# Turning a weight matrix by DMA instead of on TensorE, and what has to move for it: a gated MLP with a complex recurrence on one core

## The chip, the core and the metric

One core of one Trainium2 chip. The metric is the device time of one execution in microseconds (us). A kernel's time is the median of several executions. Engines: PE is TensorE, DVE is VectorE, ACT is ScalarE, POOL is GpSimd, SP is SyncE, which here only issues DMAs.

## The reference, cut to what matters

```python
def reference(x, Lambda_re, Lambda_im, B_re, B_im, C_re, C_im, log_dt, Dskip, w_gate, w_up, w_down):
    xn  = layernorm(x)                                   # x: 1 x 2048 x 448
    dt  = exp(log_dt);  Lam = Lambda_re + 1j*Lambda_im;  Lam_bar = exp(dt * Lam)
    Bu  = xn @ (((Lam_bar - 1) / Lam)[:, None] * (B_re + 1j*B_im)).T
    h_t = Lam_bar * h_(t-1) + Bu_t                       # over all 2048 tokens
    s   = 2 * real(h @ (C_re + 1j*C_im).T) + xn * Dskip
    g   = silu((silu(xn @ w_gate) * (xn @ w_up)) @ w_down)   # w_gate, w_up: 448 x 1792
    return x + s * g
```

## The kernel before

The tokens go in four quarters of 512 columns. Per quarter there are 14 blocks of 128 columns of `w_gate` and `w_up`, taken two at a time (a "pair": PSUM banks gp, up, gp, up). ACT empties them into `gs` and `us`, and DVE multiplies these into `Vt`. Then comes the projection Bu (banks pb and pk), the recurrence as a scan on DVE, `w_down` (bank hd) and the output sum (bank y). The recurrence is rotated by sine and cosine tables: DVE makes their phases (`table_phase`), ACT their values (`table_sin`).

In these traces an instruction that waits holds back those behind it on its engine (before the change ACT idles 1.84 us, until 23.47 us, for one of them with filled banks behind it), so the order of calls below *is* the schedule. The numbered lists are hooks: what is put into the queues behind the evictions of that pair.

```python
    for n in range(2):                      # two token tiles first
        ln_stats(n); ln_sqrt(n, n + 1); run_power()          # root: GpSimd power, then a reciprocal
    ...
    gu_matmuls(0, 0, begun, 0, W // 2, told=run_power)       # left token half of pair 0
    ...
    for d in range(0, KT, 2):
        b_transpose(0, d, nc.scalar)        # B_re: 16 PE transposes, copied out by ACT
    gu_matmuls(0, 0, begun, W // 2, W)      # right token half of pair 0
    ...
    gu(0, bg, 2.0, {
        0: [*stats(4, 5, 6, 7), *sqrt(1), on(params_in), on(table_phase, 0)],
        1: [*bs(1), on(b_clear), *rstd_of(1), *norms(4, 5, 6, 7), on(table_sin, 0)],   # bs: B_im
        2: [*transposes(4, 5, 6, 7), on(load_c), on(table_phase, 1), on(table_sin, 1),
            on(bu, 0, (0, 1)), on(table_phase, 2), on(table_sin, 2)],
        3: [on(bu, 0, (2,), "between"), on(table_phase, 3), on(table_sin, 3), on(params_fold)],
        4: [on(params_trig), on(ssm_steps, bg, 0)],
        5: [on(params_out)],
    }, begun)
```

Of the kernel before, what the change touches and what calls it, by code (L numbers as in the profile page):

```python
# [44 lines left out]
def kernel(  # L45
# [89 lines left out]


# [6 lines left out]
    def load_w(eng, eng2, dst, src, c0, c1):  # L143
        eng.dma_start(
            out=dst[:, 0:KF, c0:c1],
            in_=src[0 : KF * P, c0:c1].rearrange("(k p) f -> p k f", p=P),
        )
        eng2.dma_start(out=dst[:, KF, c0:c1], in_=src[blk(KF), c0:c1])

    def load_gu(c0, c1):  # L150
        load_w(nc.sync, nc.sync, Wg, B_w_gate, c0, c1)
        load_w(nc.sync, nc.sync, Wu, B_w_up, c0, c1)

    def load_nat(i, src):
        nc.sync.dma_start(
            out=nat[:, i, 0:KF, :], in_=src[0 : KF * P, :].rearrange("(k p) f -> p k f", p=P)
        )
        nc.sync.dma_start(out=nat[:, i, KF, :], in_=src[blk(KF), :])

    def load_turned(dst, src):  # L160

        for k, cols in ((slice(0, KF), slice(0, KF * P)), (slice(KF, KT), blk(KF))):
            nc.sync.dma_start(out=dst[:, k, :], in_=src[:, cols], transpose=True)

    nat = big.tile([P, 2, KT, D], BF16, name="nat", tag="vt")
# [19 lines left out]
    load_w(nc.sync, nc.sync, Wg, B_w_gate, 0, C0)  # L185
    load_w(nc.scalar, nc.scalar, Wu, B_w_up, 0, C0)
    load_nat(0, A_B_re)
    load_x(TQ, 2 * TQ)
    load_gu(C0, 768)
    load_nat(1, A_B_im)  # L190
    load_gu(768, F)

    nc.gpsimd.affine_select(
# [3 lines left out]
    halves = ctile([P, TQ], BF16, "halves")  # L197
    nc.gpsimd.memset(halves[:], 0.5)
    euler = ctile([P, KT], F32, "euler")
    nc.gpsimd.memset(euler[:], math.e)  # L200
    for r, v in enumerate((A_log_dt, A_Lambda_re, A_Lambda_im, A_Dskip)):
        nc.gpsimd.dma_start(out=vrow[r : r + 1, :], in_=v.unsqueeze(0))
# [21 lines left out]
    vep = ctile([P, NT], BF16, "vep")  # L224
    sd = ctile([P, NT], BF16, "sd")
# [10 lines left out]
    def ln_sqrt(n0, n1):  # L236
        power(sd[:, n0:n1], vep[:, n0:n1], halves[:, 0 : n1 - n0])

    def ln_rstd(n0, n1):
        nc.vector.reciprocal(out=rstd[:, n0:n1], in_=sd[:, n0:n1])  # L240
# [124 lines left out]
    def b_transpose(c, d, eng):  # L365

        tp = bank("tpb", BF16).rearrange("p (i w) -> p i w", i=2)
        for i in range(2):
            for k in (KF, *range(KF)):
                c0 = blk(k).start if c == 0 else (k + 1) % KT * P  # L370
                nc.tensor.transpose(  # L371
                    tp[:, i, c0 : c0 + P], nat[:, c, k, blk(d + i)], Id[:]
                )
        tp = tp[:, :, c * R : c * R + D]
        dst = BT[:, d : d + 2, c * D : (c + 1) * D]
        if eng is nc.scalar:
            nc.scalar.activation(dst, tp, ACT.Copy)
        else:
            nc.vector.tensor_copy(out=dst, in_=tp)

# [25 lines left out]
    SYNC = mybir.DependencyInfo(mybir.DependencyClass.Sync, mybir.DependencyReason.DATA)  # L406

# [9 lines left out]
    def sums(banks, weights, q, c0, c1, between=None, told=None):  # L417
# [3 lines left out]
        left = []  # L421
        for share, first in ((0, True), (1, False)):
            for n in range(len(banks)):
# [11 lines left out]
                if first:  # L435
                    left.append(tell(mm))
                    if told:
                        told()
                        told = None
# [5 lines left out]
    def bu(q, ns, packed=None):  # L445
# [15 lines left out]
        sums(pb, pairs, q, 0, W, between=whole if packed == "between" else None)  # L461
# [69 lines left out]
    def gu_banks():  # L531
        return [[bank("gp"), bank("up")] for _ in range(2)]

    def gu_matmuls(q, f0, banks, c0, c1, **kw):
        pairs = [[w[:, :, block(f)] for w in (Wg, Wu)] for f in (f0, f0 + 1)]
        sums(banks, pairs, q, c0, c1, **kw)

    def gu(q, bg, budget, hooks={}, begun=None):
# [3 lines left out]
        for f0 in range(0, NF, GRP):  # L542
# [3 lines left out]
            for i in range(0, n, 2):  # L546
                fi = f0 + i
                if begun and fi == 0:
                    banks = begun
                else:  # L550
                    banks = gu_banks()
                    gu_matmuls(q, fi, banks, 0, W)
                for j, (gp_, up_) in enumerate(banks):
                    nc.scalar.activation(gs[:, i + j, :], gp_[:], ACT.Silu)  # L554
                    nc.scalar.activation(us[:, i + j, :], up_[:], ACT.Copy)  # L555
# [54 lines left out]
    for n in range(2):  # L610
        ln_stats(n)
        ln_sqrt(n, n + 1)
        run_power()
    count_tokens()
    for n in range(2):
        ln_rstd(n, n + 1)
# [4 lines left out]
    warm(3)  # L621
    for n in range(2, TQ):
        ln_stats(n)
        ln_sqrt(n, n + 1)
    run_power()
    begun = gu_banks()
    gu_matmuls(0, 0, begun, 0, W // 2, told=run_power)
    for n in range(2, TQ):
        ln_rstd(n, n + 1)
        ln_norm(n)  # L630
    nc.scalar.activation(pcol[:], params_row(), ACT.Copy)
    ln_transpose(2, nc.vector)
    ln_transpose(3, nc.vector)
    power(dtv[:], euler[:], pcol[:, 0:KT, 0])
    for d in range(0, KT, 2):
        b_transpose(0, d, nc.scalar)
    gu_matmuls(0, 0, begun, W // 2, W)
    nc.sync.dma_start(out=Wd[:], in_=B_w_down.rearrange("(ft p) d -> p ft d", p=P))
    load_x(2 * TQ, NT)
# [11 lines left out]
    def sqrt(q):  # L651
        return [on(ln_sqrt, q * TQ, (q + 1) * TQ)]

    def rstd_of(q):
        return [on(ln_rstd, q * TQ, (q + 1) * TQ)]

    def bs(c):
# [85 lines left out]
```

## Time and profile before

| | before |
|---|---|
| median of 3 executions | 190.18 us (190.11 to 190.31) |
| span in the profile | 188.9 us (that execution took 190.72) |
| PE busy | 182.9 us, 97% |
| first gate/up matmul / end of pair 6 of quarter 0 | 7.85 us / 37.9 us |
| granted clock of PE | 1.00 |

From the page of the kernel before, the busy digits of three engines and the granted clock: the span in 40 slices of 4.7 us, tenths busy (9 is 90% or more); the first slice stands directly behind the name.

```profile
PE   7799999999999999999999999999999999999992
...
DVE  3889996799999999989999899789449999889253
ACT  3278599948999771107988632105996652302100
...
PEclk9999999999999999999999999999999999999999
```

PE's row has no hole after its second digit, so PE is the bound. DVE is nearly as full in the first half: a row of DVE put later there stays later. This row of the timeline (start us, us, engine, line, operation, tiles, idle before and what ended it) is the first step of the recurrence on DVE.

```profile
52.00 1.40 POOL L215 TENSOR_TENSOR sd<-vep,halves 128x4 bf16<-128x4 bf16 x1 [31.94 <-DVE vep L232]
```

```profile
34.00 1.23 DVE L498 TENSOR_TENSOR ere<-bu_re,CT 128x2048 bf16<-128x2048 bf16 x1 [2.33 <-ACT CT L306]
```

### The profile page before, as it was taken

The page shows a single profiled execution, that of the slowest core. Times are in us where ns is not written, and L with a number is a line of the kernel's source. Part 1 is how long each engine was busy: PE and PEld are TensorE (multiplying, and loading weights), DVE is VectorE, ACT ScalarE, POOL GpSimd, SP SyncE. Part 2 cuts the span into 40 slices and gives each one's busy share as a digit, 9 for nine tenths or more (in the row PEclk, how much of TensorE's full clock was granted, in tenths as well). Part 3 has the DMA queues.
Part 4 walks back from the last instruction along what each step waited for, and adds up shares of the span by engine and source line. Part 5 has one row for each costly group of instructions (what it writes and reads, how often), then busy time and mean ns, then how long its engine had stood idle before and what let it go on. Part 6 is the DMA issues. An engine that isn't in the chain of part 4 may idle for free.

```text
span 188.9 us, 3703 instructions
## 1 busy us (share of the span) xinstructions
PE 182.9 (97%) x1472; PEld 93.0 (49%) x1472; DVE 160.3 (85%) x267; ACT 104.0 (55%) x197; POOL 10.9 (6%) x21
## 2 busy tenths in 40 slices
PE   7799999999999999999999999999999999999992
PEld 3475434555555455544444455544444445555551
DVE  3889996799999999989999899789449999889253
ACT  3278599948999771107988632105996652302100
POOL 6422200000020000000020000000000000000000
PEclk9999999999999999999999999999999999999999
DMA  6999999100013100011005100020000000020020
GB/s 172 345 379 383 377 120 213 26 3 2 0 23 64 31 0 0 0 49 56 0 0 87 28 0 3 0 75 22 3 2 0 3 0 0 0 76 24 0 75 24
DMA packets 21121, 12.59 MB, mean 67 GB/s; under 512 B 11120, under 2 KB 20080, under 8 KB 21104
## 3 DMA queue, kind: packets, MB, share of 16 engines
q1 hardware_dynamic: 20288, 12.05, 24.3%
q10 hardware_dynamic: 688, 0.31, 0.6%
q8 instruction: 11, 0.18, 0.5%
q14 instruction: 6, 0.05, 0.1%
q0 software_dynamic: 128, 0.00, 0.0%
HBM read 8.03 MB, written 1.84 MB: 52 GB/s over the span
## 4 chain that ended last, share of the span: by engine, by line
PE 94%; DMA 2%; DVE 2%; ACT 0%; POOL 0%; issue 0%; SPq 0%; DVEq 0%
PE gp L428 24%; PE hd L567 23%; PE up L428 21%; PE y L582 11%; PE pb L428 10%; PE pk L453 2%; DMA x_all<-in_A_x_dram 2%; PE y L588 2%; PE tpb L371 1%; PE tp L259 1%; DVE ob L601 0%; DVE t L598 0%; DVE st L230 0%; ACT xT L261 0%; POOL sd L215 0%
## 5 line engine op out<-in xcount | busy, mean ns | idle before, releaser
L428 PE MATMUL gp<-xT,Wg 64*128 64x512 bf16 (+1 forms) x406 | 86.2, 369 | 0.1
L428 PE MATMUL up<-xT,Wu 64*128 64x512 bf16 (+1 forms) x406 | 85.9, 369 | 0.0
L428 PEld LDWEIGHTS <-Wg 64*128 64x128 bf16 x406 | 37.2, 94 | 23.8 <-issue 1.6
L428 PEld LDWEIGHTS <-Wu 64*128 64x128 bf16 x406 | 37.3, 94 | 19.5 <-POOLq L410 0.3
L567 PE MATMUL hd<-Wd,Vt 128*128 128x448 bf16 x224 | 43.2, 353 | 0.0
L554 ACT ACTIVATE gs<-gp 128x512 bf16<-128x512 f32 x56 | 35.1, 626 | 10.9 <-PE gp L428 7.5
L555 ACT ACTIVATE us<-up 128x512 bf16<-128x512 f32 x56 | 35.4, 633 | 0.0
L567 PEld LDWEIGHTS <-Vt 128*128 128x128 bf16 x224 | 21.8, 98 | 21.0 <-issue 0.8
L572 ACT ACTIVATE sg<-hd 128x448 bf16<-128x448 f32 x16 | 8.7, 543 | 38.3 <-PE hd L567 38.2
L559 DVE TENSOR_TENSOR Vt<-gs,us 128x2048 bf16<-128x2048 bf16 (+1 forms) x16 | 17.3, 1079 | 6.3 <-ACT us L555 6.3
L428 PE MATMUL pb<-xT,BT 64*128 64x512 bf16 x168 | 19.2, 376 | 0.0
L466 ACT ACTIVATE bu_re<-pb 128x512 bf16<-128x512 f32 x12 | 7.3, 611 | 20.9 <-PE pb L428 20.9
L598 DVE TENSOR_TENSOR t<-y,sg 128x448 f32<-128x448 f32 (+2 forms) x17 | 10.1, 595 | 10.0 <-PE y L582 9.6
L582 PE MATMUL y<-C,H_re 128*128 128x448 bf16 (+2 forms) x68 | 17.6, 342 | 0.0
L504 DVE TENSOR_TENSOR_SCAN bu_re<-rcol,H_re,ere 128x512 bf16<-128x512 f32 x12 | 15.1, 1268 | 0.0
L588 PE MATMUL y<-Dd,xT 128*128 128x128 bf16 x64 | 13.5, 212 | 0.0
L428 PEld LDWEIGHTS <-BT 64*128 64x128 bf16 x168 | 8.4, 94 | 10.1 <-issue 1.3
L582 PE MATMUL y<-C,H_im 128*128 128x448 bf16 (+2 forms) x51 | 11.9, 342 | 0.0
L230 DVE BATCH_NORM_STATS2 st<-x_all 128x6 f32<-128x448 bf16 x16 | 9.8, 616 | 2.0 <-DMA x_all<-in_A_x_dram 2.0
L504 DVE TENSOR_TENSOR_SCAN bu_im<-rcol,H_im,eim 128x512 bf16<-128x512 f32 x9 | 11.3, 1259 | 0.0
L601 DVE TENSOR_TENSOR ob<-t,x_all 128x448 bf16<-128x448 f32 (+2 forms) x17 | 10.2, 597 | 0.6
L215 POOL TENSOR_TENSOR sd<-vep,halves 128x1 bf16<-128x1 bf16 (+1 forms) x7 | 5.7, 813 | 77.8 <-PE up L428 41.8
(95 smaller groups left out, 174.9 us busy)
## 6 DMA issues: line engine op xcount, KB each, us to landing
out_dram<-ob SPq DMA_DIRECT2D x15, 112.0 KB, 1.7
Wd<-in_B_w_down_dram SPq DMA_DIRECT2D x1, 1568.0 KB, 12.0
x_all<-in_A_x_dram SPq DMA_DIRECT2D x1, 896.0 KB, 13.9
Wg<-in_B_w_gate_dram SPq DMA_DIRECT2D x1, 768.0 KB, 6.9
Wu<-in_B_w_up_dram SPq DMA_DIRECT2D x1, 768.0 KB, 8.2
x_all<-in_A_x_dram SPq DMA_DIRECT2D x1, 448.0 KB, 4.8
Wg<-in_B_w_gate_dram SPq DMA_DIRECT2D x1, 384.0 KB, 4.9
Wu<-in_B_w_up_dram SPq DMA_DIRECT2D x1, 384.0 KB, 5.3
```

Source lines behind the costliest of these rows:

```text
L230: nc.vector.bn_stats(out=st[:], in_=x_all[:, n, :])
L428: mm = nc.tensor.matmul(banks[n][i][:, c0:c1], lhsT=weights[n][i][h, d, :], rhs=xT[h, d, q * W + c0 : q * W + c1], start=(first and m == 0 ...
L504: nc.vector.tensor_tensor_scan(out=T["b"][c][:, k, :], data0=rcol[:, k : k + 1].to_broadcast([P, W]), data1=T["e"][c][:, k, :], initial=in ...
L554: nc.scalar.activation(gs[:, i + j, :], gp_[:], ACT.Silu)
L555: nc.scalar.activation(us[:, i + j, :], up_[:], ACT.Copy)
L559: nc.vector.tensor_tensor(out=Vt[:, f0 : f0 + n, :], in0=gs[:, 0:n, :], in1=us[:, 0:n, :], op=ALU.mult)
L567: nc.tensor.matmul(hd, lhsT=Vt_of[q][:, fi, j * P : (j + 1) * P], rhs=Wd[:, fi, :], start=(fi == 0), stop=(fi == NF - 1),)
L572: nc.scalar.activation(sg[:], hd, ACT.Silu)
L582: nc.tensor.matmul(y[:, c0:c1], lhsT=h, rhs=C2[:, n, c0:c1], start=(n == 0), stop=(n == NS - 1))
L588: nc.tensor.matmul(y[:, s + skip : s + P], lhsT=xT[:, n, m * P : (m + 1) * P], rhs=Dd[:, n, skip:P], start=False, stop=False,)
L598: nc.vector.tensor_tensor(out=t[:], in0=y, in1=sg[:, c0:c1], op=ALU.mult)
L601: nc.vector.tensor_tensor(out=ob[:], in0=t[:], in1=x_all[:, m, c0:c1], op=ALU.add)
```

## The change

Its intent: PE is the bound, so take B's 32 transposes off it. B comes turned from memory by transposing DMAs instead. These wait (the `gate`) until all gate/up weights have landed, so as not to slow them down. Since B then comes late, Bu of quarter 0 moves from between pairs 2, 3 and 4 to behind pair 5. To give PE work at the start without the transposes, the left token half of three blocks is done before the right half. The root is one power of -1/2 in f32 and needs no reciprocal. The first two `up` blocks are emptied by DVE.

```diff
-    load_w(nc.sync, nc.sync, Wg, B_w_gate, 0, C0)
-    load_w(nc.scalar, nc.scalar, Wu, B_w_up, 0, C0)
-    load_nat(0, A_B_re)
+    for c0, c1 in ((0, C0), (C0, 640)):
+        load_w(nc.sync, nc.sync, Wg, B_w_gate, c0, c1)
+        load_w(nc.scalar, nc.scalar, Wu, B_w_up, c0, c1)
     load_x(TQ, 2 * TQ)
-    load_gu(C0, 768)
-    load_nat(1, A_B_im)
-    load_gu(768, F)
+    load_gu(640, 1216)
+    load_b(load_gu(1216, F))
...
+    def load_b(landed):
+        gate = nc.sync.nop(nofuse=True)
+        tc.add_manual_dep(gate.ins, landed.ins.name, SYNC, reason="queue")
+        load_turned(BT, A_B_re, 0, D)
+        load_turned(BT, A_B_im[KF * P : D, :], D, R)
+        load_turned(BT, A_B_im[0 : KF * P, :], KT * P, KF * P)
...
-    def ln_sqrt(n0, n1):
-        power(sd[:, n0:n1], vep[:, n0:n1], halves[:, 0 : n1 - n0])
-    def ln_rstd(n0, n1):
-        nc.vector.reciprocal(out=rstd[:, n0:n1], in_=sd[:, n0:n1])
+    def ln_root(n0, n1):                                   # halves is -0.5, f32
+        power(rstd[:, n0:n1], vep[:, n0:n1], halves[:, 0 : n1 - n0])
...
-                    nc.scalar.activation(us[:, i + j, :], up_[:], ACT.Copy)
+                    if begun and fi == 0:
+                        nc.vector.tensor_copy(out=us[:, i + j, :], in_=up_[:])
+                    else:
+                        nc.scalar.activation(us[:, i + j, :], up_[:], ACT.Copy)
...
     gu(0, bg, 2.0, {
-        0: [*stats(4, 5, 6, 7), *sqrt(1), on(params_in), on(table_phase, 0)],
-        1: [*bs(1), on(b_clear), *rstd_of(1), *norms(4, 5, 6, 7), on(table_sin, 0)],
-        2: [*transposes(4, 5, 6, 7), on(load_c), on(table_phase, 1), on(table_sin, 1),
-            on(bu, 0, (0, 1)), on(table_phase, 2), on(table_sin, 2)],
-        3: [on(bu, 0, (2,), "between"), on(table_phase, 3), on(table_sin, 3), on(params_fold)],
-        4: [on(params_trig), on(ssm_steps, bg, 0)],
-        5: [on(params_out)],
-    }, begun)
-    gu(1, bg, 0.9, {
+        0: [*stats(4, 5, 6, 7), *root(1), on(params_in), on(table_phase, 0)],
+        1: [*norms(4, 5, 6, 7), on(table_sin, 0)],
+        2: [*transposes(4, 5, 6, 7), on(load_rest), on(table_phase, 1), on(table_sin, 1),
+            on(table_phase, 2), on(table_sin, 2)],
+        3: [on(table_phase, 3), on(table_sin, 3), on(params_fold)],
+        4: [on(params_trig)],
+        5: [on(params_out), on(b_clear), on(bu, 0, (0, 1, 2), "first"), on(ssm_steps, bg, 0)],
+    }, {0: first_pair, 1: second_pair})
+    gu(1, bg, 1.4, {
```

Cut: `first_pair` and `second_pair` (the right halves), `load_rest` (C, the last eight token tiles, `w_down`, now behind B), the parameter transposes moved ahead of the first gate/up matmul, the changed order of GpSimd's first instructions, and the removed `b_transpose`.

## The prediction

> **What bounds the kernel now.** I read the busy shares first, then the chain of work that ended last, then ScalarE (ACT) and VectorE (DVE) in order of time for 10 to 45 us, because the change reorders that stretch. From the page, busy us and the chain by engine:
> ```profile
> PE 182.9 (97%) x1472; PEld 93.0 (49%) x1472; DVE 160.3 (85%) x267; ACT 104.0 (55%) x197; POOL 10.9 (6%) x21
> ...
> PE 94%; DMA 2%; DVE 2%; ACT 0%; POOL 0%; issue 0%; SPq 0%; DVEq 0%
> ```
> TensorE (PE) is the bound: from its first gate/up matmul at 7.85 us it hardly pauses until 184.7. A busy PE could still be a waiting one, so I counted: a pair of gate/up blocks (four PSUM banks, 28 half-array matmuls, two at a time) takes 3.02 us wherever pairs follow each other undisturbed. All work from 7.85 us, at such rates, sums to 175.7 of the 176.8 us. So time is won only by taking work off PE or starting it earlier, and is lost wherever PE is made to wait. The same chain, in order of time (start us, us, what):
> ```profile
> 7.85 0.27 PE gp L428
> ...
> 10.49 0.89 PE tpb L371 x16
> ...
> 16.04 1.00 PE tpb L371 x16
> ...
> 20.17 3.02 PE pb L428 x28
> ...
> 26.21 0.86 PE pb L428 x8
> ```
> The two tpb rows are PE's transposes of B, on the path in full. The pb rows are the projection Bu of quarter 0, in two pieces between gate/up pairs 2, 3 and 4. ACT, in order of time, shows why those pieces matter:
> ```profile
> 21.01 0.62 ACT L555 ACTIVATE us<-up 128x512 bf16<-128x512 f32 x1
> 23.47 0.63 ACT L305 ACTIVATE ST<-f 128x512 bf16<-128x512 f32 x1 [1.84 <-DVE f L356]
> ...
> 26.73 0.65 ACT L305 ACTIVATE ST<-f 128x512 bf16<-128x512 f32 x1
> 27.25 0.74 ACT L306 ACTIVATE CT<-a,half_pi 128x512 bf16<-128x512 f32 x1
> 27.87 0.61 ACT L554 ACTIVATE gs<-gp 128x512 bf16<-128x512 f32 x1
> ```
> ACT empties the banks, but stands still for the sine tables until DVE has their phases. Pair 3's banks are emptied only from 27.87 us. PE didn't notice: it had Bu to do.
>
> [...]
>
> **The change part by part.**
>
> *Removed from PE's path.* 32 B transposes: 0.89 + 1.00 = 1.9 us. The parameter transposes (9.48 to 9.86) move into the idle time before the first gate/up matmul: 0.4 us. Two warm matmuls go, off the path.
>
> *The start.* One power instead of power and reciprocal saves a 0.15 us DVE row per token. Against it, ACT's queue now carries a fourth weight load that, in the built program, waits for Wg's first load (landed at 2.13 + 4.1 = 6.2 us) and takes some 0.5 us to issue, before ACT's first copy of transposed tokens (6.41 before). I call the start unchanged, 7.7 to 8.2 us. Three left halves give PE 2.3 us of work (21 pairs of 256 columns at 109 ns) and 0.45 us of token transposes while tokens 2 and 3 are normalised; the right half can begin at Tr, about 10.9 us (11.31 before). It then takes 1.53 us for two blocks, 2.29 for pair 1 and 3.02 for each further pair. Without any wait, pair 6 would end at 10.9 + 1.53 + 2.29 + 4x3.02 + 5.4 (all of Bu: 4.53 + 0.86) + 3.02 = 35.2 us; before it ended at about 37.9. **Intended gain: 2.7 us.**
>
> *B's transposing DMAs.* They wait for the last gate/up load, some 17 us (an estimate: 4.5 MB are asked for up to there; by the landing times of before 3.3 MB were in by 13.5 us and 5.4 MB by 19.4, so 0.35 MB per us). C's four took 6.2 us to issue and at most 4.8 to land, so B is there at about 25 us, hidden: Bu comes at 27 us at the earliest. C, x and w_down move back; nobody needs them before about 50 us.
>
> *DVE, and here I see the loss.* Its queue gets two evictions of up (about 0.65 us each, by the 0.62 us of reading 448 f32 columns of y from PSUM). They wait for the right half of the first pair, done for block 0 at Tr + 1.4, and all of DVE's preparation stands behind them: it begins at T0 = Tr + 2.65 = 13.55 us instead of 10.97:
> ```profile
> 10.97 0.62 DVE L230 BATCH_NORM_STATS2 st<-x_all 128x6 f32<-128x448 bf16 x1
> ...
> 23.47 0.69 DVE L357 SCALAR_TENSOR_TENSOR a<-f 128x512 f32<-128x512 f32 x1
> ...
> 25.86 0.69 DVE L357 SCALAR_TENSOR_TENSOR a<-f 128x512 f32<-128x512 f32 x1
> ```
> Table 2's phase ends 15.5 us after that start; less the copy of B, its memset and a reciprocal (17.61 to 18.58) it is 14.55. So ACT can make table 2's cosine at T0 + 14.6 = 28.15 and empty pair 3 only after it: gp at 28.85 to 29.45, up until 29.95.
>
> *PE behind it.* Pair 5 uses pair 3's banks; the built program makes it wait for exactly those evictions. With Bu moved behind pair 5, PE has nothing else: it could start pair 5 at 23.8 us and starts at 29.95. Part of those 6.1 us falls at pair 4 (pair 2 is emptied after table 0), about 1.2; some 4.9 us is one gap.
>
> *Then Bu.* Its first pb matmul waits for DVE's memset in B, which now stands behind params_out (1.48 us for its nine rows before), which waits for ACT's lam, which stands behind pair 3's evictions (1.93), table 3 (1.3) and pair 4's evictions (1.93). From 28.8: 30.75, 32.05, 34.0, lam 34.25, memset done at 35.9. Without this wait pb would start at 33.9. **2.0 us more.** Bu ends at 40.4, pair 6 at 43.4 instead of 37.9: **+5.5 us net.**
>
> *Later.* Bu's evictions end about 42.8, so DVE starts the recurrence then, not at 34.0. Its work from there to H(0) was 38.8 us without a gap; less params_out and one reciprocal 37.15: H(0) is there at 79.9 (72.9 before). PE wants it at 75.3 + 5.5 = 80.8: in time. But then DVE has 6.3 us of quarter 1's steps and two scans (2.4; one before) ahead of the four products that free y's banks: the third is done at about 92.0, and Bu of quarter 2 wants that bank at 89.9. **About 2 us more.** After that, H(1) was early by about 10 us before, so nothing follows.
>
> Sum: 190.2 + 5.5 + 2.0 = 197.7; I say **197.5 us**.
>
> **The rivals.**
>
> 1. *It works as meant*: 187.5 us. For it: PE is the bound, and 1.9 us of transposes surely go. Against it: the built order puts both cosine tables ahead of pair 3's evictions[...]. It needs DVE some 6 us earlier than its measured rows allow.
> 2. *Only the first wait*: the stall before pair 5 is there, but Bu's memset and y's banks don't bind, since DVE or ACT rows are somewhat shorter than taken. Then 190.2 - 2.7 + 6.1 = 193.6 us, to 195.6 with one of the two.
> 3. *The clock falls* in the gap of 4.9 us[...] pb waits until 35.9 anyway: mostly hidden[...].
> 4. *B lands late*: the gate opens later or transposes are slower than C's. B would have to slip by over 10 us to pass 35.9. Unlikely.
>
> **Range and chances.** The wait before pair 5 doesn't depend on when the start happens: pair 5 starts at Tr + 19.05 and could at Tr + 12.9. Its size hangs on DVE's measured rows, so I trust it to 0.5 us. The other two waits, 2 us each, are differences of long sums, and each could be 0 to 3.5. Range **194.0 to 200.5 us**. Slower by over 2% begins at 193.98: with the first wait and half of either other one it is passed. Chances: slower 0.90, within 2% 0.07, faster 0.03, the last if I misread an order.
>
> **What would show it.** In the changed profile:
> - No tpb rows; first gate/up matmul at 7.7 to 8.2 us; the right half at about 10.9.
> - DVE's statistics of token 4 start at 13 to 14 us, directly after two us copies.
> - ACT idles before tables 1 and 2 with pair 3 filled, and PE has a gap of 4 to 6 us ending near 30, released by ACT's eviction of up; PE's busy digits fall below 9 in that part (the page's slices 6 and 7).
> - Bu in one piece, its pb waiting for DVE's memset, and pair 6 ending near 43 us where it was 38.
> - A wait of PE of about 2 us near 90 us, released by DVE's product of y.
> - B's DMAs land between 22 and 28 us and nobody waits for them.
>
> It would be wrong if ACT's table rows ran ahead of the evictions, if DVE's preparation started at 11 us after all, or if the later quarters took up the delay, which I exclude because PE had no idle time there to give back.

## More of the kernel before

The POOL row of the timeline at 52.00 us is GpSimd's power for tokens 8 to 11. In `sums`, which makes the matmuls of a pair, the program lets the second half of the sums start only when the first half is done. PE is told so through GpSimd: an empty GpSimd instruction waits for the first half's last matmul, and the second half waits for that notice.

```python
    def tell(mm):                           # the notice: an empty GpSimd instruction
        told = nc.gpsimd.nop(nofuse=True)
        tc.add_manual_dep(told.ins, mm.ins.name, SYNC, reason="share")
        return told.ins.name
    ...                                     # in sums():
                if first:
                    left.append(tell(mm))
            if first:
                run_power()                 # the next power of GpSimd goes in here
```

## The result, and the profile after

The changed kernel takes **200.88 us** (median of four executions: 200.02, 200.03, 201.74, 201.93) against 190.25 (four executions) before. The ratio is 1.056, with a 95% interval of 1.049 to 1.063. Ratios are the mean time of one kernel's fast runs over that of the other's of the same rounds, so not quite the ratio of the medians quoted. The direction and the main mechanism were as predicted; the median lies 0.4 us above the range.

The times fall into two groups, near 200.0 and near 201.8. The mean granted clocks are 0.991 in the first and 0.981 to 0.983 in the second. The profile shown is of the first group. Its page, first line, busy digits, clock and chain:

```profile
PE 184.1 (93%) x1452; PEld 91.8 (46%) x1452; DVE 159.6 (81%) x260; ACT 101.5 (51%) x193; POOL 11.9 (6%) x21
...
PE   7798927999996999999999999999999999999992
...
DVE  4549988209999999999999999969929999788152
...
PEclk9999996999999999999999999999999999999999
...
PE 78%; DVE 9%; DMA 4%; ACT 3%; issue 3%; SPq 1%; DVEq 0%; POOLq 0%
```

PE's row now has a hole at slice 6 (25 to 30 us), a dent at slice 7, one at slice 13 (60 us) and a small one at slice 4. PE's share of the chain that ended last fell from 94% to 78%, and DVE's rose from 2% to 9%. The clock drops in slice 7. The holes row by row, from PE's timeline of the changed kernel:

```profile
7.31 0.21 PE L277 MATMUL tv<-Id,vrow 4*128 4x4 bf16 x3 [0.84 <-DMA vrow<-in_A_Dskip_dram]
...
10.36 0.28 PE L410 MATMUL up<-xT,Wu 64*128 64x256 bf16 x1 [0.25 <-DMA Wu<-in_B_w_up_dram]
...
18.27 0.39 PE L410 MATMUL up<-xT,Wu 64*128 64x512 bf16 x1 [0.86 <-POOLq L390]
...
30.62 0.37 PE L410 MATMUL gp<-xT,Wg 64*128 64x512 bf16 x1 [4.51 <-ACT gs L533]
...
37.10 0.39 PE L432 MATMUL pk<-xT,BT 128*128 128x512 bf16 x1 [0.37 <-DVE BT L365]
...
60.97 0.39 PE L410 MATMUL up<-xT,Wu 64*128 64x512 bf16 x1 [1.52 <-POOLq L390]
```

The parameter transposes, now ahead of the first gate/up matmul, waited 0.84 us for the parameter rows (`vrow`). The third left half waited for its weights, and pair 2 waited 0.86 us for GpSimd's queue; this last wait costs nothing here, since pair 5 waits for something else later. Pair 5 waited 4.51 us for ACT to empty pair 3. Bu waited for DVE's memset. Near 61 us PE waited 1.52 us for GpSimd's queue. ACT, from 28 us, shows what lay in front of pair 3's eviction:

```profile
28.64 0.63 ACT L303 ACTIVATE ST<-f 128x512 bf16<-128x512 f32 x1 [1.34 <-DVE f L354]
29.36 0.72 ACT L304 ACTIVATE CT<-a,half_pi 128x512 bf16<-128x512 f32 x1
29.99 0.58 ACT L533 ACTIVATE gs<-gp 128x512 bf16<-128x512 f32 x1
```

So ACT waited for table 2's phase with pair 3 full behind it. Before the change, too, pair 3 was emptied only behind table 2 (from 27.87 us, as the prediction shows); but then PE had Bu to do meanwhile. DVE, from which that phase comes, begins with the two evictions that the change gave it, and the rows of the memset and of the recurrence are late:

```profile
13.12 1.29 DVE L535 CAST us<-up 128x512 bf16<-128x512 f32 x2 [1.47 <-PE gp L410]
14.32 0.62 DVE L231 BATCH_NORM_STATS2 st<-x_all 128x6 f32<-128x448 bf16 x1
...
36.93 0.11 DVE L365 MEMSET BT<- 64x64 uint32 x1
...
44.44 1.22 DVE L477 TENSOR_TENSOR ere<-bu_re,CT 128x2048 bf16<-128x2048 bf16 x1 [7.40 <-ACT bu_re L448]
```

GpSimd's row that PE waited for at 61 us, 8.9 us later than in the kernel before:

```profile
60.93 1.41 POOL L217 TENSOR_TENSOR rstd<-vep,halves 128x4 f32<-128x4 f32 x1 [40.48 <-DVE vep L233]
```

The power waits for DVE's statistics, and PE's notice stands behind the power.

Where the time went, in the profiled executions (198.2 against 188.9 us, so 9.3):

| | before | after | lost |
|---|---|---|---|
| pair 6 of quarter 0 ends | 37.9 | 45.0 | 7.1 |
| PE behind GpSimd's queue near 61 us (1.9 us between starts, 0.2 undisturbed) | none | 1.7 | 1.7 |
| Bu of quarter 2 (pb, in the chain) | 4.64 | 4.97 | 0.3 |
| sum | | | 9.1 |

From the end of pair 6 to PE's last matmul the kernel before took 147.4 us and the changed one 149.6. This stretch, counted from the traces, is used below.

### The profile page after: what moved, and what is told of

Its sections match the earlier page's. It is cut to its first block, busy times and chain, and to the rows that moved or that the text cites. A ratio compares the mean times of both kernels' runs of the same rounds, so it can differ in the third digit from the quotient of the medians.

```text
span 198.2 us, 3659 instructions
## 1 busy us (share of the span) xinstructions
PE 184.1 (93%) x1452; PEld 91.8 (46%) x1452; DVE 159.6 (81%) x260; ACT 101.5 (51%) x193; POOL 11.9 (6%) x21
## 4 chain that ended last, share of the span: by engine, by line
PE 78%; DVE 9%; DMA 4%; ACT 3%; issue 3%; SPq 1%; DVEq 0%; POOLq 0%
PE hd L549 21%; PE up L410 17%; PE gp L410 17%; PE y L564 10%; PE pb L410 9%; DMA Wu<-in_B_w_up_dram 2%; DMA Wg<-in_B_w_gate_dram 2%; PE pk L432 2%; PE y L570 2%; DVE st L231 1%; DVE f L354 1%; DVE a L355 1%; ACT CT L304 1%; DVE xn L246 1%; ACT gs L533 1%
## 5 line engine op out<-in xcount | busy, mean ns | idle before, releaser
L410 PE MATMUL gp<-xT,Wg 64*128 64x512 bf16 (+1 forms) x413 | 88.5, 370 | 4.6 <-ACT gs L533 4.5
L410 PE MATMUL up<-xT,Wu 64*128 64x512 bf16 (+1 forms) x413 | 87.7, 371 | 2.8 <-POOLq L390 2.4
L410 PEld LDWEIGHTS <-Wu 64*128 64x128 bf16 x413 | 37.9, 95 | 29.7 <-issue 6.4
L533 ACT ACTIVATE gs<-gp 128x512 bf16<-128x512 f32 x56 | 34.2, 613 | 13.4 <-PE gp L410 10.6
L537 ACT ACTIVATE us<-up 128x512 bf16<-128x512 f32 x54 | 33.5, 620 | 0.0
L477 DVE TENSOR_TENSOR tmp<-bu_im,ST 128x2048 bf16<-128x2048 bf16 x8 | 9.8, 1219 | 3.5 <-ACT bu_im L454 3.5
L217 POOL TENSOR_TENSOR rstd<-vep,halves 128x1 f32<-128x1 f32 (+1 forms) x7 | 6.4, 911 | 91.2 <-DVE vep L233 85.4
```

What stands on the lines that cost most here:

```text
L410: mm = nc.tensor.matmul(banks[n][i][:, c0:c1], lhsT=weights[n][i][h, d, :], rhs=xT[h, d, q * W + c0 : q * W + c1], start=(first and m == 0 ...
L477: nc.vector.tensor_tensor(out=of(out, n), in0=of(a, n), in1=of(b, n), op=op)
L533: nc.scalar.activation(gs[:, i + j, :], gp_[:], ACT.Silu)
L537: nc.scalar.activation(us[:, i + j, :], up_[:], ACT.Copy)
```

## The experiments

Sixteen runs were made, of fifteen kernels (e5b repeats e5); all gave the right result. "At full clock" below means an execution with a mean granted clock of 0.996 or more.

### e1: the first evictions back to ACT

```diff
-                    if begun and fi == 0:
-                        nc.vector.tensor_copy(out=us[:, i + j, :], in_=up_[:])
-                    else:
-                        nc.scalar.activation(us[:, i + j, :], up_[:], ACT.Copy)
+                    nc.scalar.activation(us[:, i + j, :], up_[:], ACT.Copy)
```

> The changed kernel, but the two up banks of the first pair are emptied by ACT again, not by DVE. Theory (DVE's late start sets the sine tables, these set the emptying of pair 3, and this the start of pair 5): DVE's statistics of token 4 start at about 11.7 us instead of 14.3, pair 5 at about 28 instead of 30.6, the gap of PE before it shrinks from 4.5 to about 2 us, and the time falls by 2.5 to 3.5 us, to about 197 us. If the shorter gap no longer lowers the clock, the clock column stays at full and the runs no longer split into 200.0 and 201.8. Rival (the late DVE start is harmless, the banks are held up by ACT's own load): with two more evictions on ACT the time stays or rises by up to 1 us.

Measured: 196.92 us (196.71 to 197.09), ratio 1.035. DVE's statistics begin at 11.77 instead of 14.32 us, pair 5 waits 2.72 us, Bu's wait for the memset ends at 34.14 instead of 37.10. So 2.55 us of DVE's start became 3.1 to 4 us of the whole: DVE's queue sets the time here, although PE is the busiest engine.

### e2: the tables one pair later, the memset left

```diff
-        2: [*transposes(4, 5, 6, 7), on(load_rest), on(table_phase, 1), on(table_sin, 1),
-            on(table_phase, 2), on(table_sin, 2)],
-        3: [on(table_phase, 3), on(table_sin, 3), on(params_fold)],
-        4: [on(params_trig)],
-        5: [on(params_out), on(b_clear), on(bu, 0, (0, 1, 2), "first"), on(ssm_steps, bg, 0)],
+        2: [*transposes(4, 5, 6, 7), on(load_rest), on(table_phase, 1)],
+        3: [on(table_sin, 1), on(table_phase, 2)],
+        4: [on(table_sin, 2), on(table_phase, 3), on(params_fold)],
+        5: [on(params_trig), on(table_sin, 3), on(params_out), on(b_clear),
+            on(bu, 0, (0, 1, 2), "first"), on(ssm_steps, bg, 0)],
```

> The changed kernel, but ACT makes each sine table one pair later, behind the evictions of pair 3, 4 and 5 and not ahead of them; DVE's memset in B stays behind params_out. Theory (it is the order on ACT that empties pair 3 late; the second wait, for the memset, is one of its own): the gap before pair 5 is gone, pair 5 starts at about 24.7 us, but the first pb matmul then waits for the memset until about 35.5 us, so that of some 6 us only 1.5 to 2.5 are won: about 198.5 us. Rival (all of the loss is the one wait before pair 5): the time falls by 5 us or more, to 195 us or less.

Measured: 201.15 us (200.87 to 203.27), ratio 1.060. No gain, which neither side expected. PE's timeline has one wait between 19 and 60 us, and it is new:

```profile
36.29 0.61 PE L432 MATMUL pk<-xT,BT 128*128 128x512 bf16 x1 [6.17 <-DVE BT L365]
```

Pair 5 no longer waits at all, but Bu waits 6.17 us for the memset and begins only 0.8 us earlier than in the changed kernel. That is lost again to the half clock, which in this profile lies over Bu (0.50 from 34 to 40 us). The wait for the tables was real, but a second one stood behind it in parallel, nearly as late.

### e3: the memset first, the tables left

```diff
-        5: [on(params_out), on(b_clear), on(bu, 0, (0, 1, 2), "first"), on(ssm_steps, bg, 0)],
+        5: [on(b_clear), on(params_out), on(bu, 0, (0, 1, 2), "first"), on(ssm_steps, bg, 0)],
```

> The changed kernel, but DVE's memset in B stands ahead of the nine small products of params_out. Theory (Bu waits for that memset): the projection starts at about 36.3 us instead of 37.5 and everything after it 1.2 us earlier: about 199 us in the faster of the two modes. Rival (the wait is hidden, something else holds Bu): no change, 200.0 in the faster mode.

Measured: 199.81 us (198.53 to 200.83), ratio 1.050. The lowest execution is 1.5 us under the lowest of the changed kernel. PE has no wait for the memset any more; the wait before pair 5 (4.51 us) is unchanged. In the profiled execution (200.83 us) the clock was at half in two places: after the gap, and from 8.7 to 12 us at the start.

### e6 and e11: both waits, then DVE's start as well

e6 is e2 with the memset ahead of phase 3 and `params_out` behind the issue of Bu; e11 is e6 with e1's edit.

```diff
-        4: [on(table_sin, 2), on(table_phase, 3), on(params_fold)],
-        5: [on(params_trig), on(table_sin, 3), on(params_out), on(b_clear),
-            on(bu, 0, (0, 1, 2), "first"), on(ssm_steps, bg, 0)],
+        4: [on(table_sin, 2), on(b_clear), on(table_phase, 3), on(params_fold)],
+        5: [on(params_trig), on(table_sin, 3), on(bu, 0, (0, 1, 2), "first"), on(params_out),
+            on(ssm_steps, bg, 0)],
```

> The sine tables of quarter 0 one pair later (as in the run that moved them alone) AND the memset in B ahead of phase 3 and params_out, with params_out behind the issue of Bu. Moved alone, the tables gained nothing: pair 5 then had no wait at all, but Bu waited 6.17 us for the memset and began at 36.29 us instead of 37.10; and the memset alone gained some 1.5 us, because pair 5 still waited 4.51 us for evictions. My theory: the two waits lie in series behind the same late VectorE and either one alone holds Bu back to 36 to 37 us, so only both together pay. With both gone Bu begins at 30 to 31 us (the later of pair 5's end and the memset, which now ends near 30.7), ends near 36, pair 6 near 39 instead of 45.1: 192 to 194.5 us, clock at 1.00 throughout[...]. GpSimd's wait of 1.5 us near 55 us stays. Rival A: the tables and the memset only shift the wait to something else (B's last transposing DMA, the evictions of Bu): then 196 us or more, and TensorE shows one wait of 3 us or more before Bu, released by a DMA or by ScalarE. Rival B: what costs is the half clock, not the order: then the time falls only by the 1 to 3 us that the half clock takes, 197.5 to 199.

Measured: 195.39 us (194.80 to 196.06), ratio 1.027. Together the edits gain 5.5 us, where alone they gained 0 and 1.1 (by the medians). It is 0.3 to 1.6 us above the range expected: the profiled execution lost 1.32 us before its first gate/up matmul, and ran at half clock for 3.4 us from about 9.7 us. By their mean clock (0.988 to 0.991) all four executions had such a stretch, which the expectation excluded. The wait before Bu is down to 0.71 us.

> As the run with tables and memset moved, and the first pair's up blocks evicted by ScalarE again, so that VectorE's preparation starts near 11.8 us instead of 14.3. By my theory Bu then no longer waits for the memset (done near 28) and begins with the end of pair 5 or with the landing of B's last transposing DMA (28 to 30 us), whichever is later: 0.5 to 2.5 us faster than that run, 190.5 to 193 us. If B's landing binds, TensorE's wait before Bu names a DMA. Rival: ScalarE, with two more rows of 0.6 us, becomes what TensorE waits for, and the run is no faster than the other.

Measured: 191.77 us (191.38 to 193.60), ratio 1.010; 191.4 in the two executions at full clock. PE has no wait before Bu. The one wait over 0.5 us that is left after the start is GpSimd's, 1.53 us at 52.38. Pair 6 ends at 36.2 us, 1.7 us earlier than in the kernel before. So the whole loss of 7.1 us at pair 6 came from what stands in DVE's and ACT's queues and in which order, as the prediction had it. What follows pair 6 still takes 149.8 us: the kernel is slower by what it loses there.

### e8: the kernel before, with only Bu moved

```diff
         2: [*transposes(4, 5, 6, 7), on(load_c), on(table_phase, 1), on(table_sin, 1),
-            on(bu, 0, (0, 1)), on(table_phase, 2), on(table_sin, 2)],
-        3: [on(bu, 0, (2,), "between"), on(table_phase, 3), on(table_sin, 3), on(params_fold)],
-        4: [on(params_trig), on(ssm_steps, bg, 0)],
-        5: [on(params_out)],
+            on(table_phase, 2), on(table_sin, 2)],
+        3: [on(table_phase, 3), on(table_sin, 3), on(params_fold)],
+        4: [on(params_trig)],
+        5: [on(params_out), on(bu, 0, (0, 1, 2), "first"), on(ssm_steps, bg, 0)],
```

(The background budget of quarter 1 is 1.4 instead of 0.9, as in the changed kernel.)

> The kernel before with ONE thing changed: the projection Bu of quarter 0 is not spread between pairs 2, 3 and 4 but done in one piece behind pair 5, as the changed kernel does. My theory says that Bu between the pairs was the work that hid ScalarE's wait for the tables: ScalarE empties pair 3 only from 27.87 us in the kernel before, so TensorE gets a gap before pair 5, of about 4 us (pair 4 would end near 25, pair 5 can begin at about 28.5 to 29.5), and Bu comes later, which puts the recurrence back. Slower by 2 to 5 us: 192.5 to 195 us. Rival: the gap in the changed kernel comes from the late VectorE alone and not from the place of Bu: then this kernel stays within 1 us of 190.2.

Measured: 196.36 us (194.94 to 196.40), ratio 1.030; 194.94 in the one execution at full clock. So moving Bu (with that budget) costs 4.8 us against the 190.12 of the same rounds, even with B's transposes still on PE and DVE on time; but this is one execution, and the other three took 196.4. In the profiled execution, one of these, the way from the first gate/up matmul to the end of pair 6 is 3.8 us longer than before, of which the wait before pair 5 is 1.64 and half clock 1.7. What follows is 2.4 us longer, of which a wait for GpSimd at 57 us (absent before) is 1.53. The rows of PE, and the stretches from 26 us (us from start; PE busy and matmuls, granted clock, DMA share, GB/s):

```profile
27.25 0.37 PE L428 MATMUL gp<-xT,Wg 64*128 64x512 bf16 x1 [1.64 <-ACT gs L554]
```

```profile
26.00:28.00 2.00, 0.63 (x5) 1.00 0.90 166
28.00:30.00 2.00, 2.00 (x14) 0.55 0.61 119
30.00:32.00 2.00, 2.00 (x14) 0.60 0.75 155
32.00:34.00 2.00, 1.95 (x14) 1.00 0.97 194
```

The wait is 1.64 us, where the changed kernel's was 4.51, and the clock is at half behind it too, for 2 x (0.45 + 0.40) / 0.5 = 3.4 us.

### e5 and e5b: the gap filled with matmuls of zeros

```diff
+    def fill():                             # between pair 4's shares; adds zeros to its fourth bank
+        for _ in range(21):
+            nc.tensor.matmul(banks[1][1][0:R, :], lhsT=zeros[:], rhs=xT[:, 0, 0:W], start=False, stop=False)
-                    gu_matmuls(q, fi, banks, (0, W))
+                    gu_matmuls(q, fi, banks, (0, W), between=fill if begun and fi == 8 else None)
```

> The changed kernel, with 21 matmuls with weights of zero (they add zeros to a bank of pair 4 that is being summed, so the result is right) put into pair 4, 4.5 us of work in the stretch where TensorE would wait for ScalarE anyway; pair 5 waits for the same evictions as before. My theory: the granted clock falls because TensorE stands still for over 4 us; with the gap filled it stays at 1.00 from 26 to 40 us, and the two groups of times (200.0 and 201.8) become one, at 199.5 to 200.3, since in the faster group most of the half clock is hidden behind Bu's wait for the memset (37 us). Rival: the clock falls for another reason[...]: then 0.70 in 30 to 36 us stays and two groups stay. Third: the filling delays pair 4's evictions and with them everything: then over 201.9.

Measured: 201.09 us in the median of six, but one execution, the profiled one, took **398.04 us**. In it matmuls of 512 columns started every 0.44 us instead of every 0.22, from end to end, while ACT's evictions took no longer than in the changed kernel (0.60 us on average, 0.61 there). The 1.00 that its result gives as clock is no reading: this trace holds no clock record at all, and its page has no such row. Half clock throughout would fit; that is not shown, and I know no cause for it. It is left out of the comparison, and the profile can't be read for the question. The other five took 199.14 to 201.47 us with clocks of 0.998 to 0.989; the two with 0.996 and more are the two fastest (199.14, 199.73).

> The very same kernel as the run with the gap filled, whose profile fell into an execution of 398 us with every matmul at half rate, so that it can't be read; its five other executions took 199.1 to 201.5 us at clocks of 0.989 to 0.998. In all profiles so far the half clock comes in stretches of 3.4 us, one or two of them, 1.7 us of work each. My theory: with the gap filled no such stretch lies between 26 and 40 us; what is left of them lies at the start (8 to 14 us), where two other runs had one. Times between 199.1 and 199.8 without one, 201 with one. Rival: a stretch lies in 30 to 37 us as in the changed kernel although TensorE was busy there; then the gap is not its cause.

Measured: the same kernel again, 201.23 us (201.06 to 202.47), ratio 1.060. PE's row and the clock:

```profile
36.57 0.61 PE L434 MATMUL pk<-xT,BT 128*128 128x512 bf16 x1 [1.95 <-DVE BT L367]
```

```profile
30.00:32.00 2.00, 2.00 (x22) 1.00 0.36 71
32.00:34.00 2.00, 2.00 (x19) 1.00 0.49 95
34.00:36.00 2.00, 0.56 (x2) 1.00 0.90 186
36.00:38.00 2.00, 1.43 (x7) 0.62 0.98 189
38.00:40.00 2.00, 2.00 (x14) 0.53 0.63 109
```

With the gap filled, the clock is full from 26 to 36 us. But PE, no longer slowed, now stands still before Bu (1.95 us, for the memset), and the half clock follows *that* pause, over Bu itself. Neither expectation was right in full: the clock does follow the pause, but filling one pause moved it to the next. At equal mean clock (0.989 to 0.991) the three executions took 201.1 to 201.3 us, where the changed kernel took 200.0; in the profiled one the parameter transposes also waited longer, 1.29 us for 0.84, so not all of the difference is the place of the half clock.

### e4 and e12: GpSimd's power one pair later

```diff
-        2: [*stats(10, 11), *root(2), on(c_weights, 0)],
-        3: [*norms(8, 9), on(c_weights, 1)],
-        4: [*norms(10, 11), *transposes(8, 9), on(c_weights, 2)],
-        5: [*transposes(10, 11), on(c_weights, 3)],
+        2: [*stats(10, 11), on(c_weights, 0)],
+        3: [*root(2), on(c_weights, 1)],
+        4: [*norms(8, 9), on(c_weights, 2)],
+        5: [*norms(10, 11), *transposes(8, 9), on(c_weights, 3)],
+        6: transposes(10, 11),
```

e4 is this edit on the changed kernel, e12 on e11.

> The changed kernel, but the power for tokens 8 to 11 is put into GpSimd's queue one pair later, so that the notices by which PE may begin a second share do not stand behind a power that waits for DVE. Theory (PE's 1.7 us pause at 60 us is this queue): the pause at 60 us is gone. But the reading of y by DVE near 90 us waits for DVE's own work, so most of it comes back there as a wait for y's banks: PE's wait in Bu of quarter 2 grows from 0.3 to about 2 us, and the time falls by only 0 to 0.4 us. Rival (the pause is a loss of its own): the time falls by 1.7 us, to 198.3 in the faster mode.

Measured: 200.96 us (200.30 to 201.84), ratio 1.057, no gain. The wait of 1.5 us at 61 us is gone, and PE waits 0.40 and 1.04 us for y's banks instead. The times alone would not show this, since by their mean clock (0.979 to 0.983) all six executions had two stretches of half clock, and only two of the changed kernel's four had. The stretch behind pair 6 does: 149.6 us, as in the changed kernel.

```profile
92.42 0.37 PE L410 MATMUL pb<-xT,BT 64*128 64x512 bf16 x1 [0.40 <-DVE t L580]
93.84 2.53 PE L410 MATMUL pb<-xT,BT 64*128 64x512 bf16 x21 [1.04 <-DVE t L580]
```

> As the run with tables, memset and the first pair's up evictions put right (191.4 us in its full-clock executions), with GpSimd's second power one pair later as well. There, the one wait of TensorE left over 0.6 us is 1.53 us at 52.38, behind GpSimd's queue. My theory: in the changed kernel itself removing this wait gained nothing because VectorE was late and the wait came back at y's banks (0.40 + 1.04 us near 92 us); here the recurrence runs nearly as early as in the kernel before, so this time the 1.5 us are gained: 189.7 to 190.3 us in executions with the clock at 1.00 (each window of half clock adds about 1.7 us). Rival: the wait comes back at y's banks or elsewhere here too, then 191 us or more.

Measured: 191.65 us (191.47 to 193.00), ratio 1.009; 191.5 to 191.7 at full clock, e11's time. The rival was right: the same two waits (0.40 and 1.05 us) come up at 84 us, and the stretch behind pair 6 is 149.8 us in both e11 and e12. Twice, then, a wait of PE was removed and came back further down with the same releaser behind it: DVE.

### e15, e16, e17: what DVE needs

e15 is e12 with two edits: the second piece of `w_up` goes to SP's queue (the edit of e19 below), and less of the recurrence is put in front of `Vt` (`gu(0, bg, 1.2` for 2.0).

> As the run with all four put right, and two small things more. First, the fourth weight load goes from ScalarE's queue to SyncE's, so that ScalarE's first copy of transposed tokens no longer stands 4 to 5 us behind a landing load: first gate/up matmul at 7.6 to 7.9 us instead of 8.0 to 8.2, worth 0.3 us if the half-columns' loads keep up. Second, less of the recurrence is let into VectorE's queue at pair 5 (a budget of 1.2 instead of 2.0), so that the product which frees gs and us comes some 0.8 us earlier and TensorE's waits of 0.4 us in all near 43 us go. Together 0.3 to 0.8 us: 189.2 to 189.8 us at full clock, the only one of the corrected kernels that could be level with or just under the kernel before. Rival: SyncE's queue, which now carries that load, issues the right half's weights later, and the gain at the start is lost again: same time as the other run.

Measured: 190.18 us (189.41 to 190.73), ratio 1.000 (0.997 to 1.002): level with the kernel before. The first gate/up matmul is at 7.87 us. The gain over e12, 1.5 us, is larger than the 0.3 to 0.8 expected (which had e12 at 190.0, so the time itself lies 0.4 us above the range), and this in spite of a wait that is new:

```profile
74.14 0.36 PE L562 MATMUL y<-C,H_re 128*128 128x448 bf16 x1 [1.12 <-DVE H_re L478]
```

The recurrence is late because DVE stood idle twice, 2.88 us for Bu's evictions, and then for the tokens of quarter 2, whose load stands behind C's in SP's queue:

```profile
43.96 0.63 DVE L232 BATCH_NORM_STATS2 st<-x_all 128x6 f32<-128x448 bf16 x1 [1.84 <-DMA x_all<-in_A_x_dram]
```

So e16 loads these tokens right behind B and makes their statistics in the first of the two pauses:

```diff
     load_b(load_gu(1216, F))
+    load_x(2 * TQ, NT)                      # was in load_rest, behind C
...
         5: [on(params_trig), on(table_sin, 3), on(bu, 0, (0, 1, 2), "first"), on(params_out),
-            on(ssm_steps, bg, 0)],
+            *stats(8, 9, 10, 11), *root(2), on(ssm_steps, bg, 0)],
...
-        1: stats(8, 9),
-        2: [*stats(10, 11), on(c_weights, 0)],
-        3: [*root(2), on(c_weights, 1)],
+        2: [on(c_weights, 0)],
+        3: [on(c_weights, 1)],
```

> The best run so far (190.2 us), with the load of the last eight token tiles right behind B's DMAs instead of behind C's, and the statistics of tokens 8 to 11 with their power in the 2.9 us in which VectorE waited for Bu's evictions. My theory: what is left of the loss is VectorE's lateness; it gains 1.84 us (the wait for that load) and up to 2.9 us, so the waits for H (1.12 us) and for y's banks (0.46 us) vanish and nothing else appears: 188.3 to 189.0 us, faster than the kernel before by 0.6 to 1.0 per cent. Rival: TensorE's time before 35 us decides and something else takes the wait's place, such as B landing later beside the load of tokens: 190 us or more.

Measured: **187.80 us** (187.50 to 188.43), ratio **0.988** (0.985 to 0.990): faster than the kernel before by 1.2%. PE's row of the page has no hole, and its timeline shows no wait of 0.2 us or more from 4 to 130 us:

```profile
PE   7999999999999999999999999999999999999992
...
PEclk9999999999999999999999999999999999999999
```

This is more than the 1.9 us of transposes that the change was made for. Pair 6 now ends at 35.1 us, where the prediction had put it if nothing waited (35.2), and the stretch behind it takes 147.3 us, as in the kernel before. Of the gain over e15 in the profiles, 1.9 us fall in that stretch (149.2 before). The other 0.5 us lie ahead of it: the first gate/up matmul is at 7.26 us, because here the parameter transposes did not wait for their rows; e16's edit was not meant to change that.

e17 puts the parameter transposes back behind the first left halves:

> As that run, and the transposes of the four parameter rows back behind the first left halves, because there TensorE waited 0.68 us for their DMA at 7.20 us in front of the first gate/up matmul. My theory: the first gate/up matmul then follows ScalarE's copy at 7.2 to 7.5 us (7.87 before), 0.2 to 0.5 us are gained at the start, and all of VectorE's preparation comes earlier by as much: 0.2 to 0.4 us faster than the other run. Rival: the weights of the third left half (landing near 10 us) bind, and the start gains nothing.

Measured: 188.41 us (187.95 to 188.65), ratio 0.990, slower than e16 by 0.6 us. The first gate/up matmul (7.21 us) waits for ACT's copy instead, and in e16's profile the transposes had not had to wait, so the start gains nothing, and the transposes now take PE's time between matmuls (9.28 to 9.66 us).

### e19, e9 and e10: single parts

e19, the changed kernel with one load on another queue:

```diff
-        load_w(nc.scalar, nc.scalar, Wu, B_w_up, c0, c1)
+        weu = nc.scalar if c0 == 0 else nc.sync
+        load_w(weu, weu, Wu, B_w_up, c0, c1)
```

> The changed kernel with ONE thing changed: the second piece of w_up is loaded by SyncE's queue and not by ScalarE's, where it stood in front of ScalarE's first copy until another load had landed. My theory: this is why the start came late. The first gate/up matmul then comes near 7.6 us, and if the third left half gets its weights in time the right half begins near 10.9 to 11.2 us instead of 11.7; VectorE's preparation, and with it everything up to Bu, follows: 0.5 to 0.8 us faster at equal numbers of half-clock stretches, so groups near 199.4 and 201.1 instead of 200.0 and 201.8. Rival: the load lands as late from SyncE's queue (it waits for the same earlier load) and the right half still begins at 11.7: no change.

Measured: 198.93 us (198.72 to 199.30), ratio 1.046. In the changed kernel ACT's first copy of transposed tokens had waited for another weight load to land; here it did not:

```profile
6.30 1.08 ACT L259 ACTIVATE xT<-tp 128x512 bf16<-128x512 bf16 x2 [4.07 <-DMA Wg<-in_B_w_gate_dram]
```

```profile
5.66 0.60 ACT L260 ACTIVATE xT<-tp 128x512 bf16<-128x512 bf16 x1 [3.43 <-PE tp L258]
```

(first the changed kernel, then e19). The first gate/up matmul moved from 7.97 to 7.21 us, DVE's first eviction from 13.12 to 11.83, and the executions with one half-clock stretch from 200.0 to 198.7 to 199.05. The time is worth more than expected, but the 0.76 us of the first gate/up matmul is not shown to be ACT's copy alone. That copy came 0.64 us earlier; its 4.07 us of idle time are not what it lost, since the transposes that it copies were done only near 5.6 us in both. In the changed kernel PE then still waited for the parameter rows until 7.31 us, in e19 it did not; e15, with the same load on SP's queue, waited 0.68 us for them and began at 7.87. The right half began 1.29 us earlier (10.42 for 11.71), so 0.5 us more: the weights of the third left half, which are this load, landed at 8.52 us instead of 10.31, and nothing waited for them.

e9, the changed kernel without the two lines of the gate:

> The changed kernel without the gate, so that B's transposing DMAs are issued right after the weight loads. My theory: in the changed kernel nobody waits for B (it lands near 29 to 30 us and Bu waits for VectorE's memset until 37 us), so no gain: 199.7 to 200.3 and 201.4 to 202 by the clock, as before. Rival A: B's small packets, in the way of the last gate/up weights, delay these, and pairs 3 to 6 wait for a weight DMA: slower by 1 us or more. Rival B: the gate itself costs, because SyncE's queue stands behind it and the tokens' turning DMAs and w_down come late: faster by 1 us or more.

Measured: 200.14 us (199.58 to 201.50), ratio 1.053. B's DMAs are issued from 11.04 us instead of 18.59, and the waits stay: Bu still waits for the memset (0.38 us at 36.69). At the same clock (0.990 to 0.991) the three executions span 199.58 to 200.34, around the changed kernel's 200.0.

e10, the kernel before with only the root as one power (`halves` -0.5 in f32, `vep` f32, no reciprocal):

> The kernel before with ONE part of the change: the root as one power of -1/2 in f32, no reciprocal on VectorE. My theory: it takes a VectorE row of about 0.15 us (and the step to it) out of the start, so the first gate/up matmul comes at most 0.2 us earlier, and VectorE's preparation some 0.3 us; TensorE is the bound and has its work, so the time falls by 0.1 to 0.3 us (189.8 to 190.1). Rival: the power of f32 at -1/2 takes longer on GpSimd than that of bf16 at 1/2 (it was 0.57 us) and eats the gain: 190.1 to 190.4.

Measured: 189.98 us (189.96 to 190.17) against 190.17, ratio 0.9991 (0.9978 to 1.0003). That is 0.2 us in the medians, as expected, but the interval still includes no gain. The powers for tokens 4 to 11 take no longer, 1.03 and 1.41 us in f32 against 1.03 and 1.40 in bf16; the last one does, 1.99 against 1.02.

## Why the prediction was right or wrong

| | predicted | after |
|---|---|---|
| right half of the first pair begins | 10.9 | 11.71 |
| DVE: statistics of token 4 | 13.55 | 14.32 |
| ACT: cosine of table 2 begins | 28.15 | 29.36 |
| PE: pair 5 begins | 29.95 | 30.62 |
| DVE: memset in B done | 35.9 | 37.04 |
| PE: Bu ends / pair 6 ends | 40.4 / 43.4 | 42.0 / 45.0 |
| losses after that | y's banks, 2.0 | GpSimd's queue 1.7, y's banks 0.3 |

**The main mechanism was right, and runs show it.** DVE late by its two new evictions (e1: 3.1 us), tables ahead of pair 3's evictions, Bu no longer there to hide the wait (e8: 4.8 us by itself), the memset behind `params_out` (e3, e6). That nobody waits for B's DMAs was right too (no row of PE in the trace after names them, and e9), though they landed at 22.7 to 29.4 us, up to 1.4 us later than said. The chain of waits was right in its order.

**The step "The start ... I call the start unchanged ... Tr, about 10.9 us" failed**, by 0.8 us. The first gate/up matmul came at 7.97 us, inside the 7.7 to 8.2 said; the right half began at 11.71. The prediction saw that ACT's queue would hold a load that waits for another one, but counted only its issue, not its landing: the third left half waited for that load until 10.36 us, and the token transposes stood behind it. e19 moves this load, and the right half begins at 10.42; the end time falls by 1.0 to 1.3 us, since everything of DVE hangs on it (a part of this may be the parameter rows, see e19). The prediction also put the parameter transposes "into the idle time" and did not ask when their rows land: PE waited 0.84 us for them.

**The step "Table 2's phase ends 15.5 us after that start; less ... 14.55" was too short** by 0.5 us (table 2's cosine began 15.04 us after DVE's statistics, not 14.55): a scratch buffer of the phases was still being read by ACT's cosine (DVE idle for 0.52 us at 27.45 us). The rows of before were taken as a fixed sum, but one wait in it depends on where ACT stands. A further 0.4 us: not only pb but the last pk matmul as well waited for the memset. With the start's 0.8, and 0.1 us regained in between, that is the 1.6 us by which pair 6 ended later than predicted.

**The step "Later ... about 2 us more" named the wrong place and had the right size**, partly by luck. The prediction had no term for GpSimd's queue, in which PE's notices stand behind a power that waits for late DVE. That wait, 1.7 us, came first and left only 0.3 for y's banks. e4 shows that the predicted one was there: with GpSimd's wait removed it is 1.44 us. They are two faces of one lateness and don't add: behind pair 6 both kernels take 149.6 us, 2.2 more than before.

**Rival 3, "mostly hidden", was half right.** The trace of the kernel before shows no fall of the clock (1.00), so what one would cost was the author's estimate, not shown. In the changed kernel's profile the clock was at half for 2 x (0.20 + 0.50 + 0.15) / 0.5 = 3.4 us (31.2 to 34.6 us), and pair 5 ended in time for Bu to wait only 0.37 us more: hidden, as said. But half of the executions had two such stretches by their mean clock: (1 - 0.983) x 200 / 0.5 = 6.8 us of half clock, so 1.7 us more of lost work, and the median of four lies between the groups. The prediction had no term for a second stretch; on top of the 1.6 us at pair 6 and the 0.5 us of the base (below), this puts the median outside of the range. The group at 200.0 lies inside. No trace of the slower group was kept, so where its second stretch lay is not shown; in e3, at a like mean clock (0.983), it lay at the start (8.6 to 12.0 us).

**The base.** The times of the prediction came from an execution of 190.72 us, and were added to the median of 190.18: 0.5 us too low. Together: 197.7 (the sum) + 1.6 (pair 6) + 0.5 (base) + 0.0 (later) = 199.8, against 200.03 in the profiled execution.

**What stays open.** Which pauses of PE bring half a clock is settled only in part. The length of the pause alone does not decide: half clock came with pauses of 1.64 us in e8, 1.95 us in e5b, 4.51 us in the changed kernel and 6.17 us in e2, but in e1's profile, with a pause of 2.72 us, the mean granted clock was 1.00. The stretches of half clock, summed from the granted clock as above, lasted 3.4 us in the changed kernel, e5b, e6, e8, e9 and e19, and 6.8 us in e2 (2 x (0.19 + 0.50 + 0.50 + 0.50 + 0.02) / 0.5). What decides, and whether there is a limit, is not shown. The execution of 398 us is unexplained.

## What to carry to other kernels

Before work is taken off the busiest engine or moved on it, ask what that work was hiding: Bu between the pairs filled time in which PE would have had to wait for ACT, and moving it cost more than twice what the removed transposes had taken (4.8 us in e8's one execution at full clock, for 1.9). When two waits end near the same time behind the same late engine, removing either one may show little (e2 gained 0 us, e3 1.1, both together 5.5 in e6), so judge edits by the trace and try them together. When a removed wait comes back further down with the same engine behind it, stop moving waits and give that engine time: here bringing one load forward and filling a pause of DVE turned a kernel that was level with the old one into one that is 1.2% faster.
